# Fused two-problem attention: x0 and K0 loaded in halves, first Q in four PSUM banks, zero matmuls, other slots for Wq, Wo and the output projection, last stores from SP

## The chip, the cores and the metric

One core of one Trainium2 chip runs the whole kernel. The metric is the device time of one execution in microseconds (us). The kernel before takes 1211.83 us, the median of 3 runs (1210.99 to 1212.95). TensorE is called PE, VectorE DVE, ScalarE ACT, GpSimd POOL, SyncE SP.

## The reference

Two independent problems, A and B, of the same shape, are computed one after the other; the outputs stand side by side. Cut to what matters (each of A and B):

```python
B, Sq, D, H, Sk, Dh = 16, 144, 448, 16, 512, 256
q = (x @ wq).reshape(B, Sq, H, Dh).transpose(0, 2, 1, 3)
scores = einsum("bhqd,bhkd->bhqk", q, k_cache) * Dh ** -0.5
p = softmax(scores)
o = einsum("bhqk,bhkd->bhqd", p, v_cache)
out = o.transpose(0, 2, 1, 3).reshape(B, Sq, H * Dh) @ wo
```

All inputs and the output are bf16. K and V of both problems are 268 MB, so the kernel streams them once from HBM while PE computes.

## The kernel before, in words

**Units.** One unit is one (problem, batch, head): 256 units of A, then 256 of B. For each unit the kernel computes Q (L316, eight matmuls over four blocks of D, into the PSUM bank `qp_ps`), moves it to SBUF as `qt_sb` with the factor 1/16 (DVE L328 or ACT L332, by a pattern of the unit number), the scores, the softmax, its transposition, P times V (L511) and an ACT copy of the result into a ring in SBUF (L526).

**The 144 query rows are split 112 + 32.** The 112 rows of one unit are the "a" part: scores SA (L424), maximum (DVE L436), exponential (ACT L447), reciprocal (L457), normalisation (POOL L465), transposition TA (L478) and its copy (L488). The last 32 rows of four units fill 128 partitions together, the "b" part: SB (L348) does eight units at once, into two banks, with its own maximum, exponential, normalisation (L389) and transposition TB (L401).

**Loads.** K comes eight units at a time (one "K load", K0 to K63, 2.1 MB) by a transposing DMA into one of three buffers (L291). V comes four units at a time (V0 to V127, 1 MB) into one of three buffers (L301). x comes four batches at a time by two transposing DMAs (L281, L282) into one of three buffers. Wq comes in four groups of four heads (two DMAs each, L260 and L262) and B's groups overwrite A's; Wo comes in eight groups (L270). All of these are issued by SP, in one order. The stores of the output (L578) are issued by POOL.

**The output projection OP** (L549) takes the ring in chunks of 128 rows (18 chunks for each problem) and adds 32 products for each chunk ("pieces", one matmul each) into `op_ps`; ACT or DVE copies the result out (L567, L570) and the store follows. The ring holds four chunks. The last two chunks of B use two banks (`op_ps` and `qp_ps`).

**The order of the work** is written out by a planner at build time. Its loop (L659 to L753) goes through slots i. In slot i it emits, in this order: the DMAs due, exponentials and normalisations of the b part, stores, Q of unit i+15, SB if one is due (K load n has its SB in slot 8n-7), SA of unit i+5, the normalisation of unit i+4, TA of unit i+2, TB, the maxima of the b part, PV of unit i, and then OP pieces, two at a time, as long as a credit lasts. The credit grows by 2.25 pieces in each slot from slot 0 on, and is cut to 4 in slots in which no piece is queued. A chunk is queued in the slot in which its last unit's PV is emitted and is ready two slots later (`OP_DELAY`): A's chunk 0 in slot 17, chunk 1 in slot 33. Each engine runs its own instructions strictly in this order; `S.add` (L44) works out which semaphores an instruction waits for.

**The order of the loads** comes from `plan(lo, deadline, lead, ...)` (L588 to L623): loads are sorted by deadline (in slots), with ties in the order in which they were planned (x, Wq, Wo, K, V); `lo` is the first slot in which the planner may emit it, because by then the last reader of the buffer has been emitted. SP issues the loads in that order and waits at each one for the readers of its buffer. A load that waits holds back all loads behind it. Around the change from A to B (slots 224 to 257) the order before is V58, K30, V59, V60, x4, Wq group 0 of B, K31, V61, Wq 1, V62, Wq 2, K32, V63, Wq 3, V64, K33. At the start it is x0, Wq 0, Wq 1, Wq 2, K0, Wq 3, V0, K1, V1, V2, K2, then V, K and Wo by deadline, Wo between slots 12 and 26.

Of the kernel before, what the change touches and what calls it, by code (L numbers as in the profile page):

```python
# [122 lines left out]
def bass_concat_heads__mha_block_cached__gqa_block_cached__near_ridge_kernel(  # L123
# [38 lines left out]
    LSB = 7  # L162
    NK, NV, NXG = 3, 3, 3
# [3 lines left out]
    KR = 4  # L167
# [8 lines left out]
    with contextlib.ExitStack() as es:  # L176
# [29 lines left out]
        sem_names = list(COMPUTE)  # L206
# [23 lines left out]
        def t_ident():  # L230
            def e1(g):
                return g.memset(ones[:], 1.0)
            S.add(POOL, e1, writes=[("ones", 0)], name="ones")

            def e2(g):
                return g.affine_select(ident[:], ones[:], pattern=[[1, 128]], compare_op=ALU.is_equal,
                                       fill=0.0, base=0, channel_multiplier=-1)
            S.add(POOL, e2, reads=[("ones", 0)], writes=[("ident", 0)], name="ident")

# [35 lines left out]
        def t_load_x(XG):  # L275
            pr, j = divmod(XG, Bn // XB)
            sl = XG % NXG
            x = xs[pr][j * XB:(j + 1) * XB].rearrange("b q d -> (b q) d")

            def e(q):  # L280
                q.dma_start_transpose(xt_sb[:, sl, 0:3, :], x[:, 0:384]).then_inc(sems["xt%d" % sl], 16)  # L281
                return q.dma_start_transpose(xt_sb[:, sl, 3, :], x[:, 320:448]).then_inc(sems["xt%d" % sl], 16)  # L282
            S.add(SP, e, writes=[(("xt", sl), XG)], dma_sem="xt%d" % sl, n_dma=2, name="x%d" % XG)

        def t_load_k(SG):
            pr, r0 = divmod(8 * SG, NU)
            sl = SG % NK
            src = ks[pr].rearrange("b h k d -> (b h k) d")[r0 * SK:(r0 + 8) * SK, :]

            def e(q):  # L290
                return q.dma_start_transpose(kt_sb[:, sl].rearrange("p k d r -> p (k d) r"),  # L291
                                             src.rearrange("(r k) d -> r (k d)", k=KR)).then_inc(sems["kt%d" % sl], 16)
            S.add(SP, e, writes=[(("kt", sl), SG)], dma_sem="kt%d" % sl, name="k%d" % SG)
# [9 lines left out]

        def t_q(U):
# [4 lines left out]
            hg = h // 4  # L309

            def e(t):
                ins = None
                for kc in range(4):
                    for dc in range(2):
                        c0 = h * DH + dc * 128
                        ins = t.matmul(qp_ps[:, dc * SQ:(dc + 1) * SQ], lhsT=wq_sb[:, kc, c0:c0 + 128],  # L316
# [3 lines left out]
            S.add(PE, e, reads=[(("wq", hg), pr), ("wqz", 0), (("xt", xsl), XG)], writes=[("qp", ("q", U))],  # L320
                  banks=["qp"], name="Q%d" % U)

        def t_evac_q(U):
            sl = U % NQT
            src = qp_ps[:, 0:2 * SQ].rearrange("p (c q) -> p c q", c=2)
            if (U - LQ) % 8 in (2, 4, 6, 7):
                def e(v):
                    return v.tensor_scalar(qt_sb[:, sl, :, :], src, 1.0 / 16.0, None, op0=ALU.mult)  # L328
                S.add(DVE, e, reads=[("qp", ("q", U))], writes=[(("qt", sl), U)], banks=["qp"], name="eq%d" % U)
            else:  # L330
                def e(a):
                    return a.activation(qt_sb[:, sl, :, :], src, AF.Copy, scale=1.0 / 16.0)  # L332
                S.add(ACT, e, reads=[("qp", ("q", U))], writes=[(("qt", sl), U)], banks=["qp"], name="eq%d" % U)
# [5 lines left out]
        def t_sb(SG):  # L339
            ksl = SG % NK  # L340

            def e(t):
                ins = None
                for dc in range(2):
                    for jj in range(8):
                        U = 8 * SG + jj
                        j = jj % 4
                        ins = t.matmul(sb_ps[jj // 4][32 * j:32 * j + 32, :].rearrange("q (k r) -> q k r", k=KR),  # L348
                                       lhsT=qt_sb[:, U % NQT, dc, QA:SQ],
                                       rhs=kt_of(U, dc), start=(dc == 0), stop=(dc == 1),  # L350
                                       tile_position=(0, 32 * j))
                return ins
            S.add(PE, e, reads=[(("qt", (8 * SG + jj) % NQT), 8 * SG + jj) for jj in range(8)] + [(("kt", ksl), SG)],
                  writes=[(("sbb", 0), ("s", 2 * SG)), (("sbb", 1), ("s", 2 * SG + 1))], banks=["sb0", "sb1"],
# [61 lines left out]
        def t_sa(U):  # L416
# [11 lines left out]
            S.add(PE, e, reads=[(("qt", U % NQT), U), (("kt", ksl), SG)], writes=[(("sap", bank), ("s", U))],  # L428
# [41 lines left out]
        def t_ta(U):  # L470
            psl = U % NPA
            bank = U % 2
# [10 lines left out]
        def t_evac_pta(U):  # L483
            sl = U % NPT
            bank = U % 2
# [87 lines left out]
        def t_store(r):  # L573
            pr, row0, m = chunk_rows(r)
            sl = r % NOST

            def e(q):
                return q.dma_start(of[row0:row0 + m, pr * D:(pr + 1) * D], ost_sb[0:m, sl, :]).then_inc(  # L578
                    sems["ost%d" % sl], 16)
            S.add(POOL, e, reads=[(("ost", sl), r)], dma_sem="ost%d" % sl, name="st%d" % r)  # L580
# [4 lines left out]
        t_ident()  # L585
        dma_plan = []
# [4 lines left out]
        s_min = -LQ - 24  # L591
        for XG in range(NXGT):
            pr, j = divmod(XG, Bn // XB)
            u_first = pr * NU + j * XB * H
            dl = u_first - LQ
# [5 lines left out]
            plan(lo, dl, 40, t_load_x, XG)  # L601
        for pr in range(NP):
            for hg in range(HG):
                dl = pr * NU + 4 * hg - LQ
                lo = pr * NU - H + 4 * hg + 3 - LQ + 1 if pr > 0 else s_min
                plan(lo, dl, 10 ** 6, t_load_wq, pr, hg)
        for wg in range(NWG):
            plan(s_min, H - 4 + 2 * wg, 10 ** 6, t_load_wo, 0, wg)
        for SG in range(NSG):
            dl = 8 * SG - LSB  # L610
            lo = 8 * (SG - NK) + 7 - LS + 1 if SG >= NK else s_min
            plan(lo, dl, 12, t_load_k, SG)
        for G in range(NG):
            dl = 4 * G
# [27 lines left out]
        OP_RATE = float(NCH * NWO) / NU  # L642
# [16 lines left out]
        while True:  # L659
# [3 lines left out]
            sgi, ph = divmod(i + LSB, 8)  # L663
            do_sb = ph == 0 and 0 <= sgi < NSG
            ga, gb = 2 * sgi, 2 * sgi + 1
            ok = 0 <= sgi < NSG
            if ok and ph == 1:
                t_exp_b(ga)
            if ok and ph == 3:
                t_exp_b(gb)  # L670
            if ok and ph == 2:
                t_recip_b(ga)
                t_norm_b(ga)
            if ok and ph == 4:
                t_recip_b(gb)
                t_norm_b(gb)
            while stores and stores[0][1] <= i:
                t_store(stores.pop(0)[0])
            if do_sb and sgi == 0:
                t_sb(sgi)  # L680
            u = i + LQ
            if 0 <= u < NT:
# [125 lines left out]
```

## Time and profile before

| | |
|---|---|
| median of 3 runs | 1211.83 us (1210.99 to 1212.95) |
| the profiled execution | 1210.82 us |
| its span (first to last instruction) | 1209.1 us |
| PE busy | 1174.4 us, 97% of the span |
| DVE, ACT, POOL busy | 64%, 62%, 56% |
| DMA | 294.15 MB, mean 243 GB/s |
| first matmul | 10.33 us |
| last matmul ends | 1202.5 us |

The span is the time from the first to the last of the program's own instructions; 1.7 us of the execution lie around it. Busy times are sums over the span, so they say which engine is full, and not where a wait is: for this, the waits and the order of time are read stretch by stretch. "Idle before" in a line is the time for which the engine stood still ahead of that instruction, and the name behind the arrow is what ended it.

### The profile page before, as it was taken

What the parts mean: (1) busy time and instruction counts of PE and PEld (TensorE: products, weight loads), DVE (VectorE), ACT (ScalarE), POOL (GpSimd) and SP (SyncE); (2) the same over time, 40 slices, a digit from 0 to 9 for tenths busy, and PEclk for the clock granted to TensorE, in tenths of its full rate; (3) what the DMA queues carried; (4) which work ended last, traced back from release to release, by engine and by line L of the source; (5) the groups of instructions that cost most, each with busy time, mean ns of one, the idle gap of its engine ahead of it and who ended that gap; (6) DMA issues with size and microseconds to landing.
All of it is one profiled execution on the core that took longest, in us unless ns stands there. A gap on an engine that the chain in (4) does not pass through costs nothing.

```text
span 1209.1 us, 33868 instructions
## 1 busy us (share of the span) xinstructions
PE 1174.4 (97%) x13952; PEld 894.2 (74%) x13952; DVE 770.1 (64%) x2179; ACT 753.7 (62%) x2213; POOL 678.5 (56%) x682
## 2 busy tenths in 40 slices
PE   4898999999999999999999999999999999999997
PEld 3676777777777777777777777777777777777765
DVE  1765666666666666666666666666666666666563
ACT  1665666666666666666666666666666666666553
POOL 0555565565555565565555655655655655665553
PEclk9999999999999999999999999999999999999999
DMA  9999999999999999999999999998999999999971
GB/s 249 281 285 289 245 252 225 245 251 247 246 235 237 231 259 226 246 246 232 290 283 282 284 272 265 228 258 225 245 244 236 224 249 244 242 240 234 232 178 47
DMA packets 627033, 294.15 MB, mean 243 GB/s; under 512 B 548416, under 2 KB 556608, under 8 KB 626880
## 3 DMA queue, kind: packets, MB, share of 16 engines
q1 hardware_dynamic: 625152, 287.85, 101.8%
q0 software_dynamic: 1728, 4.13, 1.1%
q8 instruction: 111, 1.82, 0.6%
q14 instruction: 42, 0.34, 0.1%
HBM read 148.90 MB, written 4.13 MB: 127 GB/s over the span
## 4 chain that ended last, share of the span: by engine, by line
PE 90%; DMA 5%; DVE 3%; SPq 1%; ACT 0%; issue 0%; POOL 0%; ACTq 0%
PE qp_ps L316 20%; PE ot_ps L511 19%; PE sa_ps L424 19%; PE op_ps L549 17%; PE sa_ps L478 8%; PE sb_ps L348 5%; DMA kt_sb<-in_A_k_cache_dram 3%; PE sb_ps L401 2%; DMA kt_sb<-in_B_k_cache_dram 2%; DVE stat L436 1%; DMA wq_sb<-in_A_wq_dram 0%; DVE pt_sb L488 0%; PE qp_ps L549 0%; DVE pt_sb L410 0%; DVE qt_sb L328 0%
## 5 line engine op out<-in xcount | busy, mean ns | idle before, releaser
L465 POOL TENSOR_TENSOR pa_sb<-pa_sb,stat 112x512 bf16<-112x512 bf16 x512 | 531.8, 1039 | 490.8 <-DVE stat L457 490.7
L447 ACT ACTIVATE pa_sb<-sa_ps,stat 112x512 bf16<-112x512 f32 x512 | 352.1, 688 | 408.0 <-DVE stat L436 407.0
L436 DVE TENSOR_REDUCE stat<-sa_ps 112x1 f32<-112x512 f32 x512 | 353.9, 691 | 324.6 <-PE sa_ps L424 321.1
L316 PE MATMUL qp_ps<-xt_sb,wq_sb 128*128 128x144 bf16 x4096 | 344.1, 228 | 16.1 <-DMA wq_sb<-in_A_wq_dram 10.3
L316 PEld LDWEIGHTS qp_ps<-xt_sb,wq_sb 128*128 128x128 bf16 x4096 | 290.5, 99 | 93.1 <-issue 11.1
L511 PE MATMUL ot_ps<-pt_sb,v_sb 128*128 128x144 bf16 x4096 | 340.4, 226 | 0.0
L424 PE MATMUL sa_ps<-kt_sb,qt_sb 128*112 128x512 bf16 x1024 | 310.9, 385 | 1.0 <-DVE pt_sb L488 0.8
L549 PE MATMUL op_ps<-wo_sb,ring 128*128 128x448 bf16 x1120 | 278.8, 352 | 0.0
L511 PEld LDWEIGHTS ot_ps<-pt_sb,v_sb 128*128 128x128 bf16 x4096 | 268.5, 97 | 0.4
L478 PEld LDWEIGHTS sa_ps<-ident,pa_sb 112*128 112x128 bf16 x2048 | 145.0, 97 | 111.3 <-ACT pa_sb L447 24.9
L526 ACT ACTIVATE ring<-ot_ps 128x288 bf16<-128x288 f32 (+8 forms) x512 | 190.3, 372 | 4.4 <-PE ot_ps L511 4.4
L488 DVE COPY pt_sb<-sa_ps 128x448 bf16<-128x448 bf16 x512 | 190.7, 372 | 2.4 <-PE sa_ps L478 2.4
L478 PE MATMUL sa_ps<-ident,pa_sb 112*128 112x112 bf16 x2048 | 185.4, 212 | 0.1
L328 DVE TENSOR_SCALAR qt_sb<-qp_ps 128x288 bf16<-128x288 f32 x256 | 117.0, 457 | 96.5 <-PE qp_ps L316 93.9
L389 POOL TENSOR_TENSOR pb_sb<-pb_sb,stat 128x512 bf16<-128x512 bf16 x128 | 132.8, 1037 | 27.1 <-DVE stat L381 27.1
L332 ACT ACTIVATE qt_sb<-qp_ps 128x288 bf16<-128x288 f32 x256 | 106.0, 414 | 35.0 <-PE qp_ps L316 32.5
L424 PEld LDWEIGHTS sa_ps<-kt_sb,qt_sb 128*112 128x112 bf16 x1024 | 97.0, 129 | 38.8 <-issue 26.7
L549 PEld LDWEIGHTS op_ps<-wo_sb,ring 128*128 128x128 bf16 x1120 | 95.1, 98 | 27.6 <-ACT ring L526 0.2
L447 ACT ACTIVATION_READ_ACCUMULATOR pa_sb<-sa_ps,stat 112x1 f32 x512 | 98.9, 193 | 0.0
L361 DVE TENSOR_REDUCE stat<-sb_ps 128x1 f32<-128x512 f32 x128 | 87.2, 681 | 3.7 <-PE sb_ps L348 3.7
L371 ACT ACTIVATE pb_sb<-sb_ps,stat 128x512 bf16<-128x512 f32 x128 | 88.5, 691 | 0.0
L457 DVE RECIPROCAL stat<-stat 112x1 f32<-112x1 f32 x512 | 78.4, 153 | 0.5 <-ACT pa_sb L447 0.5
(23 smaller groups left out, 366.1 us busy)
## 6 DMA issues: line engine op xcount, KB each, us to landing
v_sb<-in_A_v_cache_dram SPq DMA_DIRECT2D x64, 1024.0 KB, 6.1
v_sb<-in_B_v_cache_dram SPq DMA_DIRECT2D x64, 1024.0 KB, 6.0
out_dram<-ost_sb POOLq DMA_DIRECT2D x36, 112.0 KB, 5.1
wo_sb<-in_A_wo_dram SPq DMA_DIRECT2D x8, 448.0 KB, 6.3
wo_sb<-in_B_wo_dram SPq DMA_DIRECT2D x8, 448.0 KB, 6.2
wq_sb<-in_A_wq_dram SPq DMA_DIRECT2D x4, 768.0 KB, 6.7
wq_sb<-in_B_wq_dram SPq DMA_DIRECT2D x4, 768.0 KB, 7.6
wq_sb<-in_A_wq_dram SPq DMA_DIRECT2D x4, 128.0 KB, 6.9
```

The lines of the kernel that those rows point to most:

```text
L316: ins = t.matmul(qp_ps[:, dc * SQ:(dc + 1) * SQ], lhsT=wq_sb[:, kc, c0:c0 + 128], rhs=xt_sb[:, xsl, kc, xo:xo + SQ], start=(kc == 0 and dc ...
L328: return v.tensor_scalar(qt_sb[:, sl, :, :], src, 1.0 / 16.0, None, op0=ALU.mult)
L389: return g.tensor_tensor(pb_sb[:, psl, :], pb_sb[:, psl, :], stat[:, RINVB + sl:RINVB + sl + 1].to_broadcast([128, SK]), op=ALU.mult)
L424: ins = t.matmul(sa_ps[bank][0:QA, :].rearrange("q (k r) -> q k r", k=KR), lhsT=qt_sb[:, U % NQT, dc, 0:QA], rhs=kt_of(U, dc), start=(dc = ...
L436: return v.tensor_reduce(stat[0:QA, NEG + sl:NEG + sl + 1], sa_ps[bank][0:QA, :], axis=AX.X, op=ALU.max, negate=True)
L447: return a.activation(pa_sb[0:QA, psl, :], sa_ps[bank][0:QA, :], AF.Exp, bias=stat[0:QA, NEG + sl:NEG + sl + 1], scale=1.0, accum_out=stat ...
L465: return g.tensor_tensor(pa_sb[0:QA, psl, :], pa_sb[0:QA, psl, :], stat[0:QA, RINV + sl:RINV + sl + 1].to_broadcast([QA, SK]), op=ALU.mult)
L478: ins = t.transpose(pta_ps[bank][:, c * 128:c * 128 + QA], src[:, c, :], ident[0:QA, 0:QA])
L488: return v.tensor_copy(pt_sb[:, sl, :, 0:QA], pta_ps[bank][:, 0:512].rearrange("p (c q) -> p c q", c=4)[:, :, 0:QA])
L511: ins = t.matmul(ot_ps[ob][:, dc * SQ:(dc + 1) * SQ], lhsT=v_sb[:, vsl, j, c * DH + dc * 128:c * DH + (dc + 1) * 128], rhs=pt_sb[:, sl, c, ...
L526: ins = a.activation(ring[:, 2 * h:2 * h + 2, c0:c0 + n1], src[:, :, 0:n1], AF.Copy)
L549: ins = t.matmul(acc[0:m, 0:D], lhsT=ring[:, c, col0:col0 + m], rhs=wo_sb[:, c, :], start=(c == first), stop=(c == last))
```

## The change

- **Loads at the start.** x0 and K0 are loaded in two halves each, with semaphores of their own for the first halves. The order becomes x0 first half, Wq 0, K0 first half, Wq 1, K0 second half, V0, Wq 2, Wq 3, K1, V1, V2, K2, V3, Wo 0, Wo 1, V4, x0 second half, K3, V5, Wo 2, Wo 3, V6, K4, Wo 4, Wo 5, V7, V8, Wo 6, Wo 7, K5, V9 and so on.
- **Q of the first units.** Units 0 to 7 use four PSUM banks in turn, units 8 to 31 two; the slots of the first 32 Q are set by a table, as are those of SB0, SB1, SB2 (slots -5 and -1, 4, 10) and SA of unit 8 (slot 4). SB0 is split in two.
- **Zero matmuls.** 12 matmuls on zeros ahead of the first Q and 8 behind the first four, into a bank that nothing else uses then.
- **Wq of B** gets the deadlines 232, 236, 240 and 244 in place of 241, 245, 249 and 253. Sorted, the order around the change from A to B becomes V57, Wq 0, V58, K30, Wq 1, V59, Wq 2, V60, x4, K31, Wq 3, V61, V62, K32, V63, V64, K33.
- **Output projection.** A's chunks are ready in slot 34 at the earliest; the credit grows by 2.5 in each slot.
- **Last stores.** The two last chunks are stored by SP with semaphores of their own, and SP waits for them at its end.

```diff
+    WO_AT = (15, 21, 27, 33)
+    OP_FROM = (34, 0)
+    N_WARM = (12, 8)
...
+        def t_warm_zero():
+            def e(v):
+                return v.memset(pt_sb[:, 0, :, :], 0.0)
+            S.add(DVE, e, writes=[("warm", 0)], name="warmz")
...
+        def q_bank(U):
+            four = ((qp_ps, "qp", "qp"), (op_ps, "opp", "op"), (ot_ps[0], ("otp", 0), "ot0"),
+                    (ot_ps[1], ("otp", 1), "ot1"))
+            if U < 8:
+                return four[U % 4]
+            return four[U % 2] if U < 32 else four[0]
...
+        def t_warm(k):
+            def e(t):
+                ins = None
+                for _ in range(N_WARM[k]):
+                    ins = t.matmul(sb_ps[1][:, :], lhsT=ident[:, :], rhs=pt_sb[:, 0, :, 0:128], start=True, stop=True)
+                return ins
...
-            S.add(POOL, e, reads=[(("ost", sl), r)], dma_sem="ost%d" % sl, name="st%d" % r)
+            S.add(SP if r in tail_chunks else POOL, e, reads=[(("ost", sl), r)], dma_sem=sem, name="st%d" % r)
...
+        sb_slot = [8 * n - LSB for n in range(NSG)]
+        sb_slot[0:3] = [-LS, 4, 10]
+        sa_slot = [u - LS for u in range(NT)]
+        sa_slot[8] = 4
+        q_slot = [u - LQ for u in range(NT)]
+        q_slot[0:32] = [-5] * 4 + [-3, -3, -2, -2] + [1] * 4 + [2] * 4 + [4, 5, 5, 6, 7, 8, 9, 9] + \
+            [10, 11, 11, 12, 13, 14, 15, 16]
...
+            if XG == 0:
+                plan(s_min, -60, 0, t_load_x, 0, (0,))
+                plan(s_min, q_slot[2 * H], 40, t_load_x, 0, (1,))
...
-                dl = pr * NU + 4 * hg - LQ
+                dl = pr * NU - H + 4 * hg + 7 - LQ if pr > 0 else (-59, -57, -55, -53)[hg]
                 lo = pr * NU - H + 4 * hg + 3 - LQ + 1 if pr > 0 else s_min
...
-            plan(s_min, H - 4 + 2 * wg, 10 ** 6, t_load_wo, 0, wg)
+            plan(s_min, WO_AT[wg // 2], 10 ** 6, t_load_wo, 0, wg)
...
+            if SG == 0:
+                plan(s_min, -58, 0, t_load_k, 0, (0,))
+                plan(s_min, -56, 0, t_load_k, 0, (1,))
...
-            dl = 4 * G
+            dl = 4 * G if G > 0 else -55.5
...
-        OP_RATE = float(NCH * NWO) / NU
+        OP_RATE = 10.0 / 9 * NCH * NWO / NU
...
-                            queue_chunk(r, i + OP_DELAY)
+                            queue_chunk(r, max(i + OP_DELAY, pr * NU + OP_FROM[pr]))
...
+                if eng_name == SP:
+                    for k in range(len(tail_chunks)):
+                        eng.wait_ge(sems["ostt%d" % k], 16)
```

## The prediction

> **What bounds the kernel now.** I read the chain that ended last, the waits of PE, the stretches of the start, the order of time around the change from A to B, and the end.
>
> ```profile
> PE 90%; DMA 5%; DVE 3%; SPq 1%; ACT 0%; issue 0%; POOL 0%; ACTq 0%
> ```
>
> PE sets the time. An edit pays where PE stands idle and costs where it makes PE wait. PE's waits of over 0.3 us, by cause:
>
> ```profile
> PE qp_ps L316 <- DMA wq_sb<-in_A_wq_dram: 10.3, 1, 10.3
> PE sb_ps L348 <- DMA kt_sb<-in_A_k_cache_dram: 6.1, 4, 1.9
> PE qp_ps L316 <- DVE qt_sb L328: 3.1, 6, 0.6
> PE qp_ps L316 <- ACT qt_sb L332: 2.6, 5, 0.6
> PE sb_ps L348 <- DMA kt_sb<-in_B_k_cache_dram: 2.9, 2, 2.2
> ```
>
> The four K waits in A are SB2 to SB5, at 56.49, 73.76, 94.47 and 112.87 us; the two in B are SB32 and SB33. The stretches between the first six of these SBs (span, PE, PEld, DVE, ACT, POOL, clock, DMA share, GB/s):
>
> ```profile
> 23.60:39.00 15.40, 12.43 (x128) 7.93 (x128) 8.93 (x24) 7.27 (x21) 6.61 (x7) 1.00 1.14 271
> 39.00:56.40 17.40, 15.75 (x201) 11.89 (x200) 11.89 (x35) 11.95 (x36) 10.76 (x11) 1.00 1.19 277
> ...
> 94.40:112.80 18.40, 16.48 (x206) 12.60 (x206) 11.94 (x34) 11.61 (x33) 10.91 (x11) 1.00 1.15 284
> ```
>
> The DMA share is above 1 in all of them, and SP issues without a pause until 125 us. So until SB5 (slot 33) the kernel runs at the pace of the DMA queue, and K5's arrival near 112.8 us is the gate. How many OP pieces PE had done by then:
>
> ```profile
> 0.00:112.87 112.87, 7.69 (x32) 2.78 (x32) 1.00 1.13 272
> 112.87:132.40 19.53, 6.22 (x26) 2.26 (x26) 1.00 1.12 265
> 132.40:148.94 16.54, 1.46 (x6) 0.52 (x6) 1.00 1.20 243
> ```
>
> From SB6 on PE is full. The next place is the reload of Wq. All K loads, issue to landing, and SP around them:
>
> ```profile
> DMA to landing us min/median/max: 11.4/15.2/20.2
> ```
>
> ```profile
> 537.79 7.37 SPq L301 DMA_DIRECT2D v_sb<-in_A_v_cache_dram  x2
> 545.21 12.97 SPq L291 DMA_TRANSPOSE kt_sb<-in_A_k_cache_dram  x1
> ...
> 568.62 0.58 SPq L260 DMA_DIRECT2D wq_sb<-in_B_wq_dram  x1
> 569.24 0.51 SPq L262 DMA_DIRECT2D wq_sb<-in_B_wq_dram  x1
> 569.80 9.92 SPq L291 DMA_TRANSPOSE kt_sb<-in_A_k_cache_dram  x1
> ```
>
> K30 is issued at 545.21, K31 at 569.80. PE at Q243 (slot 228), SB30, Q251 (slot 236) and SB31:
>
> ```profile
> 554.88 0.66 PE L316 MATMUL qp_ps<-xt_sb,wq_sb 128*128 128x144 bf16 x8
> 565.98 1.05 PE L348 MATMUL sb_ps<-kt_sb,qt_sb 128*32 128x512 bf16 x16
> ...
> 572.90 0.66 PE L316 MATMUL qp_ps<-xt_sb,wq_sb 128*128 128x144 bf16 x8
> 583.51 1.05 PE L348 MATMUL sb_ps<-kt_sb,qt_sb 128*32 128x512 bf16 x16
> ```
>
> **The start: nothing is gained by SB5.** Q in four banks takes away the eleven waits for copies (3.1 + 2.6 us); the zero matmuls can let the first Q run at the fast clock (eight cold ones span 1.12 to 1.14 us until 26.5 us, 0.67 us after); the smaller first loads bring Q0 forward by at most x0's second halves, under 1 us. All that stands ahead of K1, and the gate behind it is DMA. By K5 the same bytes must land as before: x0, all of Wq, all of Wo (groups 6 and 7 sort just ahead of K5), K0 to K5, V0 to V8. PE is not the bound: eight slots without OP take 16.54 - 6 x 0.15 = 15.6 us (0.15 us for a piece: 2.99 us less in the third OP row than in the second, for 20 pieces less); from slot 1 at some 28 us, slot 33 could come at 28 + 4 x 15.6, some 90 us. So these edits are worth 0, with some 20 us of idle PE ahead of SB5 as cover; the 20 zero matmuls (128x512, 0.385 us mean, up to double cold, at most 15 us, 12 of them ahead of Q0 in PE's empty 10.3 us) and the memset on DVE (the similar one took 1.76 us) lie in it too. K0 and x0 in parts add three small DMAs and one more change between copies and transposes. No row shows this alone: below nothing if the mix runs better, above two times 1.9 us (a small store, issue to landing). I take **+1.3**.
>
> **OP moved behind slot 33.** Before, 32 pieces are done while PE waits for K. Now none is ready until slot 34. The credit piles up from slot 15 on (a chunk is queued), to 4 + 20 x 2.5 = 54, so chunk 0 comes as a burst of 32 in slot 34, chunk 1 in slots 36 to 38. By slot 49 both kernels have done 64 pieces, so those 32 move from idle PE time to full PE time: 32 x 0.15 = 4.8 to 32 x 0.19 = 6.1 us (ten in a row took 1.89 us). I take **+6.0**. The rate of 2.5 after that moves the same pieces about, on a full PE: 0.
>
> **Wq of B: a new wait on SP.** Wq 0 now stands ahead of V58 and K30 and waits for Q243, its buffer's last reader, which ends at 555.5. Before, nothing held V58 and K30 beyond V58's own buffer, and K30 went at 545.21. Now Wq 0 (0.58 + 0.51), V58 (0.58) go first and K30 is issued near 556.9; SB30 needs it at 565.98, 9.1 us later. Even the shortest landing, 11.4, is late; with the median 15.2 PE waits **+6.1** (bounds 2.3 and 11.1). The same again: Wq 2 waits for Q251, 9.9 us ahead of SB31, and behind it come V60, x4 and K31. Before, the issues of V60, x4 and Wq 0 took from 562.96 to 569.80, so K31 goes some 7 us after Q251, near 580.5, and lands 13.5 later at best of that stretch, 10.5 us late; without the Wq that lay ahead of it then, some 8. I take **+9.0** (6 to 14). Behind it Wq 3, V61, V62 and K32 are one Wq less than before, so the waits of 2.2 and 0.7 us at SB32 and SB33 go: **-2.9**. V60 and x4 land before K31; they add no wait.
>
> **The clock after these waits.** Granted clock at the end (the third number from the right):
>
> ```profile
> 1202.50:1207.50 5.00, 0.03 (x1) 0.00 (x0) 0.62 (x1) 0.29 (x1) 1.12 (x2) 1.00 0.12 46
> 1207.50:1209.10 1.60, 0.00 (x0) 0.00 (x0) 0.00 (x0) 0.00 (x0) 0.00 (x0) 0.51 0.00 0
> ```
>
> The last matmul ends at 1202.5, and 5.0 us later the clock is halved. Waits of 6 and 9 us are longer. At the start some 3.2 us of dense work (SB0 at 23.69 and the Q behind it) passed before Q ran in 0.67 in place of 1.14 us, so a cold start loses 3.2 x (1 - 0.67/1.14) = 1.3 us. Two: **+2.6**, bounds 0 and 6. [...]
>
> **The end.**
>
> ```profile
> L176 POOLq DRAIN  x1: 3006/3006/3006, 1205.9 to 1205.9; - x1
> ```
>
> DVE's last copy ends at 1203.27. POOL issues both stores (1203.09, 1.12 us), they land by 1205.6, then POOL alone needs 3.0 us to drain, and the span ends. With the stores on SP, whose own drain took 0.13 us, POOL's drain follows its last normalisation (1196.04) and is covered by PE's work until 1202.5. SP issues at about 1202.9 and 1203.4, landing 1.9 later as on POOL, plus 0.5: 1205.9. **-3.2**; bounds -3.4 and -0.2 (POOL's median landing of 5.1). SP's queue is empty then. [...]
>
> **Sum.** 1.3 + 6.0 + 6.1 + 9.0 - 2.9 + 2.6 - 3.2 = +18.9. On the profiled execution: 1210.82 + 18.9 = 1229.7. The median of the runs lies 1.0 above it: **1230.7**.
>
> **Rivals.**
> 1. *The shorter start reaches the end.* K5 lands some 7 us earlier, for instance because copies and transposes disturb each other less. For: 23.6 us pass before SB0. Against: same bytes, queue full. 1230.7 - 7 = 1224.
> 2. *The Wq waits are hidden:* K30 and K31 arrive in time. Then 6.1, 9.0 and 2.6 go: 1213. Against: no K landed within 11.4 us.
> 3. *Faster: K lands faster.* One mechanism: a K landing in its shortest 11.4 us and no longer in some 18 (SB2 to SB5 before), because smaller groups of copies stand ahead. Place: the queue up to K5, then K30 and K31. K5 would come when PE is ready, up to 18 us earlier, PE's floor there being some 95; the mid waits become 2.3 and some 7: -18 + 6.0 + 9.3 - 2.9 - 3.2 = -8.8, so 1203. Between 18 and 11.4 the sum turns negative near 13.5. Against: the rows of 271 to 284 GB/s show no gaps to be filled.
> 4. *Worse:* K30 and K31 take the longest landings (11 + 14), SB5 starts cold too: 1230.7 + 10 + 2 = 1243.
> That the change doesn't do what it says is not one of them: the order of loads follows from its deadlines.
>
> **Chances.** Forecast 0.62, rival 1 0.13, rival 2 0.10 (half of it within 0.2%, half above), rival 3 0.08, rival 4 0.07. Two runs' medians can be told apart from about 0.2% on. So faster 0.08, same 0.05, slower 0.87. The range takes in rivals 1 and 4 and the lower bounds of the mid waits, and leaves out rival 3 and part of 2: 1215 to 1243.
>
> **What would show it.** SB5 at 112 to 116 us with no OP ahead of it, and 30 or more OP matmuls in a row behind it; SP waiting before B's first Wq until Q243; PE waits on K of 2 us or more at SB30 and 6 or more at SB31, none at SB33; Q in 1.1 us just after them; two stores on SP and a span that ends some 2.6 us after DVE's last copy. An SB5 before 108 us, or K30 landing before SB30, would make the forecast wrong.

## The result and the profile after

The changed kernel takes 1240.48 us, the median of 5 runs (1239.3 to 1241.8), beside 1212.38 us (5 runs, 1210.99 to 1214.93) for the kernel before. The ratio is 1.0231, with a 95% interval of 1.0216 to 1.0246: it is 28 us slower. The forecast was 1230.7 us, 18.9 us slower. The profiled execution takes 1241.8 us with a span of 1240.1 us, 31.0 us more than the one before. It is the slowest of its kernel's runs, and the profiled one before lies below all five of its own, so the 31.0 us that are split up below are 2.9 more than the medians differ by. Line numbers move: in the changed kernel Q is L339, SB L381, SA L455, TA L509, PV L542, OP L580, the zero matmuls L367, K loads L307, V loads L316, Wq L268 and L270, stores L610.

The chain that ended last, by engine:

```profile
PE 87%; DMA 6%; SPq 3%; DVE 3%; issue 0%; ACT 0%; POOL 0%; DVEq 0%
```

PE's share fell from 90% to 87%, and SP's queue, at 1% before, now has 3%: some of the way to the end leads through SP's issues. PE's waits for DMA (the view of waits: engine, tile and line, what ended the wait, then us in total, times, longest):

```profile
PE sb_ps L381 <- DMA kt_sb<-in_A_k_cache_dram: 25.1, 6, 6.5
...
PE qp_ps L339 <- DMA wq_sb<-in_A_wq_dram: 3.9, 3, 2.6
...
PE qp_ps L339 <- DMA xt_sb<-in_B_x_dram: 2.4, 1, 2.4
...
PE ot_ps L542 <- DMA v_sb<-in_A_v_cache_dram: 1.6, 1, 1.6
```

K of A cost 6.1 us of waits before and 25.1 now: 12.7 of these stand ahead of SB30 and SB31, the other 12.4 at the start. The 10.3 us for the first Wq, in which PE stood empty before, are gone from this row, since the zero matmuls stand there; the last two rows are new. The order of time of PE at the places that matter (start, duration, operation, then in brackets the idle time before it and what ended it):

```profile
111.74 1.90 PE L381 MATMUL sb_ps<-kt_sb,qt_sb 128*32 128x512 bf16 x16 [2.11 <-DMA kt_sb<-in_A_k_cache_dram]
...
117.13 6.22 PE L580 MATMUL op_ps<-wo_sb,ring 128*128 128x448 bf16 x32
...
566.58 0.66 PE L339 MATMUL qp_ps<-xt_sb,wq_sb 128*128 128x144 bf16 x8
...
585.05 1.90 PE L381 MATMUL sb_ps<-kt_sb,qt_sb 128*32 128x512 bf16 x16 [6.55 <-DMA kt_sb<-in_A_k_cache_dram]
...
593.15 0.66 PE L339 MATMUL qp_ps<-xt_sb,wq_sb 128*128 128x144 bf16 x8
...
603.72 0.67 PE L542 MATMUL ot_ps<-pt_sb,v_sb 128*128 128x144 bf16 x8 [1.64 <-DMA v_sb<-in_A_v_cache_dram]
606.75 1.12 PE L339 MATMUL qp_ps<-xt_sb,wq_sb 128*128 128x144 bf16 x8 [2.37 <-DMA xt_sb<-in_B_x_dram]
614.02 1.90 PE L381 MATMUL sb_ps<-kt_sb,qt_sb 128*32 128x512 bf16 x16 [6.15 <-DMA kt_sb<-in_A_k_cache_dram]
```

The rows are SB5, the burst of chunk 0, Q243, SB30, Q251, the PV that needed V60, the first Q that needed x4, and SB31. SB32 and SB33 have no wait. OP's pieces by stretch (the stretch and its length, then busy us and count of PE and of PEld, which are PE's weight loads, then the granted share of PE's full clock, DMA share, GB/s) show none ahead of SB5 and 64 in the 28 us behind it:

```profile
0.00:111.70 111.70, 0.00 (x0) 0.00 (x0) 0.95 1.12 274
111.70:140.00 28.30, 12.76 (x64) 6.12 (x64) 0.94 0.74 179
```

SP's queue at the reload of Wq: first what its Wq loads waited for (the view of waits), then its order of time:

```profile
SPq L268 <- PE qp_ps L339: 25.1, 2, 16.1
```

```profile
567.28 0.37 SPq L268 DMA_DIRECT2D wq_sb<-in_B_wq_dram  x1
567.69 0.51 SPq L270 DMA_DIRECT2D wq_sb<-in_B_wq_dram  x1
568.24 1.50 SPq L316 DMA_DIRECT2D v_sb<-in_A_v_cache_dram  x1
569.78 13.15 SPq L307 DMA_TRANSPOSE kt_sb<-in_A_k_cache_dram  x1
...
593.84 0.37 SPq L268 DMA_DIRECT2D wq_sb<-in_B_wq_dram  x1
594.25 0.50 SPq L270 DMA_DIRECT2D wq_sb<-in_B_wq_dram  x1
594.79 0.59 SPq L316 DMA_DIRECT2D v_sb<-in_A_v_cache_dram  x1
595.43 5.39 SPq L292 DMA_TRANSPOSE xt_sb<-in_B_x_dram  x1
600.86 2.86 SPq L293 DMA_TRANSPOSE xt_sb<-in_B_x_dram  x1
603.76 8.07 SPq L307 DMA_TRANSPOSE kt_sb<-in_A_k_cache_dram  x1
```

The two waits are those for Q243, which ends at 567.24, and for Q251, which ends at 593.81. K30 (569.78) and K31 (603.76) each go out behind a Wq that had waited for its buffer's last Q; K31 has V60 and x4 ahead of it too, and x4 alone holds the queue for 8.3 us.

Where the 31 us arise is read by comparing the start of each SB in both traces, at SBs ahead of which both have done equally many OP pieces:

```
place    pieces done   before     after     lag      grown since the row above
SB7            64      148.94    156.32    + 7.4     + 7.4  start, OP moved
SB29          448      547.81    558.14    +10.3     + 3.0  nothing but the rate of OP
SB33          512      622.30    651.6     +29.3     +19.0  reload of Wq
SB61         1024     1131.04   1165.5     +34.5     + 5.2  nothing but the rate of OP
end of span           1209.1    1240.1     +31.0     - 3.5  last stores
```

The forecast had +7.3, 0, +14.8 with the clock, 0 and -3.2 in these rows. Two of them are off: the reload by 4 us and the rate by 8.

### The profile page after: what moved, and what is told of

The parts are those of the page before. It is cut to its first block, busy times and chain, and to the rows that moved or that the text cites. A ratio compares the mean times of both kernels' runs of the same rounds, so it can differ in the third digit from the quotient of the medians.

```text
span 1240.1 us, 33914 instructions
## 1 busy us (share of the span) xinstructions
PE 1195.1 (96%) x13972; PEld 893.8 (72%) x13972; DVE 771.5 (62%) x2180; ACT 747.9 (60%) x2213; POOL 676.3 (55%) x680
## 4 chain that ended last, share of the span: by engine, by line
PE 87%; DMA 6%; SPq 3%; DVE 3%; issue 0%; ACT 0%; POOL 0%; DVEq 0%
PE sa_ps L455 19%; PE ot_ps L542 18%; PE qp_ps L339 18%; PE op_ps L580 17%; PE sa_ps L509 7%; DMA kt_sb<-in_A_k_cache_dram 6%; PE sb_ps L381 5%; PE sb_ps L432 2%; DVE stat L467 1%; SPq L307 1%; SPq L292 1%; DVE pt_sb L519 1%; DVE pt_sb L441 1%; PE qp_ps L580 0%; SPq L293 0%
## 5 line engine op out<-in xcount | busy, mean ns | idle before, releaser
L542 PE MATMUL ot_ps<-pt_sb,v_sb 128*128 128x144 bf16 x4096 | 341.6, 226 | 1.6 <-DMA v_sb<-in_A_v_cache_dram 1.6
L339 PE MATMUL qp_ps<-xt_sb,wq_sb 128*128 128x144 bf16 x3952 | 328.8, 226 | 6.5 <-DMA wq_sb<-in_A_wq_dram 3.9
L339 PEld LDWEIGHTS qp_ps<-xt_sb,wq_sb 128*128 128x128 bf16 x3952 | 276.0, 98 | 65.5 <-DMA wq_sb<-in_A_wq_dram 5.4
L455 PE MATMUL sa_ps<-kt_sb,qt_sb 128*112 128x512 bf16 x1024 | 316.1, 391 | 1.6 <-DVE pt_sb L519 1.4
L542 PEld LDWEIGHTS ot_ps<-pt_sb,v_sb 128*128 128x128 bf16 x4096 | 269.6, 98 | 2.2 <-DMA v_sb<-in_A_v_cache_dram 1.8
L580 PE MATMUL op_ps<-wo_sb,ring 128*128 128x448 bf16 x1120 | 265.4, 353 | 0.0
L509 PEld LDWEIGHTS sa_ps<-ident,pa_sb 112*128 112x128 bf16 x2048 | 140.6, 97 | 120.3 <-ACT pa_sb L478 46.1
L509 PE MATMUL sa_ps<-ident,pa_sb 112*128 112x112 bf16 x2048 | 186.3, 213 | 1.5 <-ACT pa_sb L478 1.1
L352 DVE TENSOR_SCALAR qt_sb<-qp_ps 128x288 bf16<-128x288 f32 x243 | 111.0, 457 | 87.2 <-PE qp_ps L339 84.3
L455 PEld LDWEIGHTS sa_ps<-kt_sb,qt_sb 128*112 128x112 bf16 x1024 | 96.8, 130 | 49.8 <-issue 30.1
L580 PEld LDWEIGHTS op_ps<-wo_sb,ring 128*128 128x128 bf16 x1120 | 98.2, 98 | 42.9 <-ACT ring L557 0.2
L381 PE MATMUL sb_ps<-kt_sb,qt_sb 128*32 128x512 bf16 x1024 | 71.4, 401 | 27.3 <-DMA kt_sb<-in_A_k_cache_dram 25.1
```

The lines of the kernel that those rows point to most:

```text
L339: ins = t.matmul(acc[:, dc * SQ:(dc + 1) * SQ], lhsT=wq_sb[:, kc, c0:c0 + 128], rhs=xt_sb[:, xsl, kc, xo:xo + SQ], start=(kc == 0 and dc = ...
L381: ins = t.matmul(dst.rearrange("q (k r) -> q k r", k=KR), lhsT=qt_sb[:, U % NQT, dc, QA:SQ], rhs=kt_of(U, dc), start=(dc == 0), stop=(dc = ...
L455: ins = t.matmul(sa_ps[bank][0:QA, :].rearrange("q (k r) -> q k r", k=KR), lhsT=qt_sb[:, U % NQT, dc, 0:QA], rhs=kt_of(U, dc), start=(dc = ...
L509: ins = t.transpose(pta_ps[bank][:, c * 128:c * 128 + QA], src[:, c, :], ident[0:QA, 0:QA])
L542: ins = t.matmul(ot_ps[ob][:, dc * SQ:(dc + 1) * SQ], lhsT=v_sb[:, vsl, j, c * DH + dc * 128:c * DH + (dc + 1) * 128], rhs=pt_sb[:, sl, c, ...
L580: ins = t.matmul(acc[0:m, 0:D], lhsT=ring[:, c, col0:col0 + m], rhs=wo_sb[:, c, :], start=(c == first), stop=(c == last))
```

## Experiments

In the table the ratio is that of each kernel's runs to those of the kernel before on the same chip (1212.9 to 1214.0 us), with its 95% interval. Names beginning with "a" start from the changed kernel, those with "b" and "c" from the kernel before.

| run | edit | us | ratio |
|---|---|---|---|
| a1_wq_back | changed kernel, Wq of B in the old order | 1229.62 | 1.0135 (1.0115 to 1.0154) |
| a2_op_early | changed kernel, OP and Wo early again | 1234.77 | 1.0175 (1.0157 to 1.0193) |
| a3_rate_back | changed kernel, rate 2.25 | 1233.58 | 1.0167 (1.0147 to 1.0188) |
| a4_start_and_stores | all three back: start and stores remain | 1211.29 | 0.9980 (0.9967 to 0.9993) |
| a5_no_zero_matmuls | a4 without zero matmuls | 1210.25 | 0.9975 (0.9964 to 0.9986) |
| b1_stores | last stores on SP alone | 1211.45 | 0.9979 (0.9965 to 0.9993) |
| b2_rate_4p5 | rate 4.5 alone | 1262.19 | 1.0399 (1.0372 to 1.0425) |
| b3_wq_even | Wq deadlines evened out | 1216.38 | 1.0020 (1.0006 to 1.0034) |
| b4_spread | two pieces in every slot | 1205.64 | 0.9935 (0.9914 to 0.9956) |
| c2_spread_stores_even | b4, b1 and b3 | 1203.09 | 0.9910 (0.9883 to 0.9937) |
| c3_wq3_earlier | c2, last Wq earlier | 1201.97 | 0.9901 (0.9872 to 0.9931) |
| c4_fill | b4, b1 and a backlog spent at the reload | 1195.71 | 0.9840 (0.9825 to 0.9856) |

### Taking the parts back one at a time

**a1_wq_back** gives Wq of B its old deadlines again:

```diff
-                dl = pr * NU - H + 4 * hg + 7 - LQ if pr > 0 else (-59, -57, -55, -53)[hg]
+                dl = pr * NU + 4 * hg - LQ if pr > 0 else (-59, -57, -55, -53)[hg]
```

> The changed kernel with one edit: B's Wq groups get the deadlines of before (241, 245, 249, 253). Theory (SP waits at Wq 0 and Wq 2 for Q243 and Q251, and V58, K30, V60, x4 and K31 stand behind them): from SB29 to SB33 the changed kernel lost 19.0 us (10.3 behind before at SB29, 29.3 at SB33), and this comes back, so 1240.5 - 19 = 1221.5; K waits at SB30 and SB31 gone, about 2.9 us at SB32 and SB33 again. Rival (the reload's 3.7 MB are what delays K, wherever they stand in the order): under 5 us come back, 1236 or more.

Some 12 us come back in the runs, not 19. SB30 has no wait any more, but SB31 and its neighbours do (PE's order of time):

```profile
579.51 1.05 PE L381 MATMUL sb_ps<-kt_sb,qt_sb 128*32 128x512 bf16 x16
598.77 1.90 PE L381 MATMUL sb_ps<-kt_sb,qt_sb 128*32 128x512 bf16 x16 [3.39 <-DMA kt_sb<-in_A_k_cache_dram]
621.33 1.05 PE L381 MATMUL sb_ps<-kt_sb,qt_sb 128*32 128x512 bf16 x16 [0.58 <-DMA kt_sb<-in_B_k_cache_dram]
638.42 1.05 PE L381 MATMUL sb_ps<-kt_sb,qt_sb 128*32 128x512 bf16 x16 [1.22 <-DMA kt_sb<-in_B_k_cache_dram]
```

From SB29 to SB33 its lag still grows by 4.7 us (11.4 to 16.1). At rate 2.5 only 2 pieces lie between SB30 and SB31, where the kernel before has 14. So PE gets to SB31 sooner, and K31, which stands behind V59 and V60 and these behind earlier PVs, lands only at 598.63. So rate and reload are not independent, and the expectation, which took the terms for additive, missed.

**a2_op_early** and **a3_rate_back** take back the floor of slot 34 (with Wo's old slots) and the credit:

```diff
-    OP_FROM = (34, 0)
+    OP_FROM = (0, 0)
...
-            plan(s_min, WO_AT[wg // 2], 10 ** 6, t_load_wo, 0, wg)
+            plan(s_min, H - 4 + 2 * wg, 10 ** 6, t_load_wo, 0, wg)
```

```diff
-        OP_RATE = 10.0 / 9 * NCH * NWO / NU
+        OP_RATE = float(NCH * NWO) / NU
```

> The changed kernel with A's chunks ready two slots after their last PV again (no floor of slot 34) and Wo's deadlines of before (12 to 26), which the earlier pieces need. Theory (32 pieces done while PE waits for K before SB5 are free): the 8.5 us lost between SB5 and SB7 come back apart from the cold start at SB5, so 1240.5 - 7 = 1233.5, with SB5 within 3 us of 111.7. Rival (Wo's groups ahead of K3 and K4 make these late, so that what OP gains the K waits take): 1239 or more, with SB5 at 115 or later.

> The changed kernel with the credit of before (2.25 in each slot). Theory (a slot without OP pieces takes 1.78 us, one with two 2.01, and each two more 0.38, so the first two pieces of a slot cost 0.15 us less than others, and each slot left empty loses 0.15): the planner leaves 186 slots empty at 2.5 and 115 at 2.25, so 71 x 0.15 = 10.6 us at most, some 8 after the slots that lie in waits: 1240.5 - 9 = 1231.5. Rival (the prediction's: PE is full, and the rate moves the same pieces about): 1240.5; the lag that grows from SB7 to SB29 and from SB33 to SB61 then has another cause.

Both came out within about 2 us. With OP early, SB5 comes at 114.70 (3.0 later than in the changed kernel, with 32 pieces already done) and the lag at SB7 is 2.0 us instead of 7.4. Wo's place was taken back together with OP's, so the two are not told apart. With the old rate the lag stands still: +7.93 at SB7 and +7.88 at SB29, +25.4 at SB33 and +25.6 at SB61. So the rate alone makes the drift, on an engine that both profiles show as full. Windows from SB7 to SB29, first of the kernel before, then of the changed one (the columns as above, with DVE, ACT and POOL behind PEld):

```profile
148.94:547.81 398.87, 398.57 (x4785) 304.95 (x4786) 263.83 (x748) 258.19 (x766) 232.50 (x232) 1.00 1.05 242
```

```profile
156.32:558.14 401.82, 401.42 (x4784) 303.84 (x4785) 264.01 (x748) 256.14 (x766) 232.50 (x233) 1.00 1.04 240
```

The same work on every engine, PE busy for all but 0.3 and 0.4 us, and 2.95 us more in the second. The busy share doesn't show this: it is 99.9% in both. The weight loads for TA do: their waits for ACT's exponential, in the view of waits, of the kernel before, of the changed one, of a3, and of b2 and b4 below, which have many and few slots without pieces:

```profile
PEld sa_ps L478 <- ACT pa_sb L447: 24.9, 88, 0.6
```

```profile
PEld sa_ps L509 <- ACT pa_sb L478: 46.1, 155, 1.6
```

```profile
PEld sa_ps L509 <- ACT pa_sb L478: 27.2, 91, 1.6
```

```profile
PEld sa_ps L478 <- ACT pa_sb L447: 84.0, 305, 0.6
```

```profile
PEld sa_ps L478 <- ACT pa_sb L447: 7.2, 27, 0.3
```

The slots without pieces in these five kernels are 102, 186, 115, 357 and 26, and the waits stand in them: 83 of the 102 in the kernel before and 150 of the 186 in the changed one have one, of the slots with pieces 2 and 3. One of them, in a stretch of the changed kernel without pieces (PEld's order of time):

```profile
594.20 0.22 PEld L509 LDWEIGHTS sa_ps<-ident,pa_sb 112*128 112x128 bf16 x4 [0.28 <-ACT pa_sb L478]
```

I also took the time from each PV to the next in the trace of PE, for slots without SB or TB, and its median by the number of OP pieces between them (12 from the changed kernel, the others from the kernel before; its two slots with 8 lie at the end, where no Q is left):

```
pieces in the slot      0       2       4       6       10      12
us from PV to PV      1.781   2.010   2.389   2.766   3.524   3.902
```

From 2 pieces on, each pair costs 0.378 us. The first pair costs 0.229. So a slot without pieces loses 0.149 us. With the waits above, I read this as PE's own work there being shorter than the chain SA, maximum (DVE), exponential (ACT), TA, copy (DVE), next SA, whose steps use the two `sa_ps` banks in turn. In the two stretches in which nothing but the spread of OP's pieces differs, the empty slots, their difference from the kernel before times 0.149 us, and the growth of the lag (us) go together in each of these kernels (b4 does two pieces fewer in the first stretch):

```
                  SB7 to SB29                  SB33 to SB61
          empty   x 0.149    lag       empty   x 0.149    lag
before      36                           19
a3          36       0.0    - 0.1        19       0.0    + 0.2
changed     57     + 3.1    + 3.0        58     + 5.8    + 5.2
b2         125     +13.3    +13.9       154     +20.1    +20.6
b4           0     - 5.4    - 5.0         0     - 2.8    - 2.6
```

**a4_start_and_stores** takes back all three (the two diffs above and that of a1). What remains is the start in halves with its zero matmuls, and the stores.

> The changed kernel with B's Wq deadlines, the floor of slot 34, Wo's deadlines and the credit all as before, so that what is left of the change is the start (halves, slots, four banks, zero matmuls) and the last stores. Theory (K5 is the gate in both, the start gains nothing by SB5 and the split adds 1 to 2 us of DMA time): SB5 at 113 to 115 us, SB7 some 2 us behind before, the end 3.5 us shorter: 1.5 us below before, ratio 0.999. Rival (the earlier first Q reaches the end once the losses are gone): SB5 and SB7 some 5 us ahead of before, ratio 0.993.

The time held: 0.998. SB5, behind the same 32 pieces as before, comes at 114.28, 1.40 us late, and SB7 is late by as much. So the start alone gains nothing by SB5, as forecast, although SB0's first half begins at 13.04 us here and SB0 at 23.69 before. The reason given did not hold in this profile. K5 is issued at 95.15 and lands 15.0 us later, at 110.17, 2.6 us ahead of the kernel before. PE is not there: it is busy throughout, and SB5 has no wait (a window, all engines, then PE's order of time):

```profile
94.00:112.00 18.00, 18.00 (x231) 13.99 (x227) 12.93 (x38) 11.92 (x34) 11.01 (x12) 1.00 1.17 304
```

```profile
114.28 1.05 PE L381 MATMUL sb_ps<-kt_sb,qt_sb 128*32 128x512 bf16 x16
```

The waits for K have moved ahead and become fewer and longer: 3.99 us at SB1 and 4.18 at SB3, each followed by 6.83 us at half the clock, where the kernel before has four of 1.1 to 1.9 us at SB2 to SB5 and no half clock behind them. So PE's cover ahead of SB5 is used up; in a5, where K5 lands at 113.76, SB5 does wait for it. From SB29 to SB33 this profile loses 2.3 us more, with a wait of 3.87 us at SB32 (2.19 before, 2.90 in b1, which loads as before).

**a5_no_zero_matmuls** also takes out the zero matmuls (PE then does nothing ahead of Q0):

```diff
-            if i == q_slot[0]:
-                t_warm(0)
...
-            if i == q_slot[0]:
-                t_warm(1)
```

> As a4_start_and_stores, without the 20 zero matmuls. Theory (they only warm a stretch that lies ahead of a K wait of 4 us at SB1): same SB1, SB2 and SB3 to 0.5 us, same time within 1 us as a4_start_and_stores, with the first Q in 1.1 us in place of 0.67. Rival (without them the clock stays cold until 26 us as in before and SB1 or SB2 come late): 2 to 5 us more.

The first Q takes 1.12 us instead of 0.67, as expected. SB2 and SB3 come 1.1 and 1.7 us earlier than in a4, not within 0.5; the changed kernel and a1, with the same program up to there, differ by 1.3 and 1.4 us at these places, so this tells nothing. In time the two intervals overlap almost wholly (0.9967 to 0.9993 and 0.9964 to 0.9986): no effect of the zero matmuls can be told from none. The other parts of the start (halves, banks, slots) were not tested one by one.

### One part alone, on the kernel before

**b1_stores** (the two stores' semaphores and SP's wait for them at its end are not shown):

```diff
...
-            S.add(POOL, e, reads=[(("ost", sl), r)], dma_sem="ost%d" % sl, name="st%d" % r)
+            S.add(SP if r in tail_chunks else POOL, e, reads=[(("ost", sl), r)], dma_sem=sem, name="st%d" % r)
...
```

> The kernel before with the last two stores on SP and nothing else. Theory (POOL's drain of 3.0 us ends the span of before; on SP it is covered): 3.5 us less, 1212.4 - 3.5 = 1208.9. Rival (a store from SP takes longer to land than on POOL, or the drain follows all the same): within 0.5 us of before.

2.5 us are gained in the runs (0.0021 of 1213.6, by the interval 0.8 to 4.2); 3.5 were expected and lie within. In the profiled execution the end saves 3.6 us, but SB63 is 1.1 us late: 0.4 us of it arises before SB5, and the wait at SB32 is 2.90 instead of 2.19. Neither can come from a store at the end, so single profiles scatter by about 1 us here. The end itself is read in the changed kernel: DRAINs (duration in ns, start in us), then SP's stores.

```profile
L179 POOLq DRAIN  x1: 3756/3756/3756, 1229.7 to 1229.7; - x1
```

```profile
1237.42 0.83 SPq L610 DMA_DIRECT2D out_dram<-ost_sb  x2
```

POOL's drain of 3.76 us is over at 1233.5, while PE still has matmuls until 1237.1. The two stores land at 1239.12 and 1239.59, 1.7 us after their issue, and the span ends 0.5 us later.

**b2_rate_4p5** exaggerates the rate:

```diff
-        OP_RATE = float(NCH * NWO) / NU
+        OP_RATE = 2.0 * NCH * NWO / NU
```

> The kernel before with the credit doubled to 4.5 pieces in each slot, nothing else. Theory (each slot without pieces loses 0.15 us, since the first two pieces of a slot cost 0.23 us together and any further two 0.38): the planner leaves 357 slots empty in place of 102, 255 x 0.15 = 38 us more, ratio 1.031. Rival (the prediction's: on a full PE the rate moves the same pieces about): within 1 us of before.

The direction and most of the size held (49 us instead of 38). What the expectation left out is at the start (PE's order of time): at this rate OP asks for Wo before it has come.

```profile
82.84 0.55 PE L549 MATMUL op_ps<-wo_sb,ring 128*128 128x448 bf16 x2 [1.19 <-DMA wo_sb<-in_A_wo_dram]
...
97.09 1.67 PE L549 MATMUL op_ps<-wo_sb,ring 128*128 128x448 bf16 x4 [9.08 <-DMA wo_sb<-in_A_wo_dram]
```

That makes SB5 11.2 us late; from there to SB61 the lag grows by 39.6 us, of which one wait of 3 us is for K31. Of its slots 357 have no pieces, 255 more than before: 255 times 0.149 is 38. Stretch by stretch it agrees too (the table under a3).

**b3_wq_even** tests whether evenly placed Wq groups take away the waits at SB32 and SB33:

```diff
-                dl = pr * NU + 4 * hg - LQ
+                dl = (235, 239, 246, 253)[hg] if pr > 0 else 4 * hg - LQ
```

> The kernel before with B's Wq deadlines 235, 239, 246 and 253, so that Wq 0 stands behind K30, Wq 1 behind V59, Wq 2 behind V61, Wq 3 behind V63: two groups are loaded earlier than before, but none ahead of a K load that is due sooner than the Q it waits for lets through. Theory (it is the place ahead of V58, K30 and K31 that hurts, not the early load): no wait at SB30 and SB31 over 0.5 us, the wait of 2.2 us at SB32 gone, since one Wq group less lands between K31 and K32: 2 to 3 us less than before, ratio 0.998. Rival (any earlier load of Wq delays K, because the DMA queue is full there): waits of 2 us or more at SB30 or SB31, ratio 1.002 or more.

The rival held: the kernel becomes slower, by 0.2% (0.06 to 0.34%). The waits at SB32 and SB33 go, and one of 5.16 us at SB31 takes their place (PE's order of time):

```profile
589.92 1.90 PE L348 MATMUL sb_ps<-kt_sb,qt_sb 128*32 128x512 bf16 x16 [5.16 <-DMA kt_sb<-in_A_k_cache_dram]
```

K31 lands at 589.79. In the kernel before it lands at 583.31, 0.2 us ahead of SB31: there was no slack for one more Wq group in front of it. By the trace of SP, V59 has gone by 561.4, Wq 1 goes out at 565.14, when its Q is done, and V60 behind it at 566.10; before, V60 went at 562.96, which is 564.3 with the 1.3 us by which this run is late already. So some 1.8 us go to Wq 1 on SP. The larger part is behind it: the issue of x4 takes 10.1 us instead of 5.2. Wq 0 and Wq 1, 1.8 MB, now stand ahead of x4, where before none did; that this is the reason is likely, but no run shows it by itself.

### Versions that use what was found

**b4_spread** gives every slot two pieces, and four where more than 34 are ready:

```diff
-                credit += OP_RATE
+                credit = 2.0 + (2.0 if sum(1 for x in fifo["op"] if x[2] <= i) > 34 else 0.0)
...
-                            op_hold = i + 2
+                            op_hold = i + 1
```

> The kernel before with two pieces in every slot in which any is ready, four when more than 34 wait, and the next chunk one slot after the last in place of two. Theory of the empty slots: 26 slots stay empty in place of 102, 76 x 0.15 = 11.3 us less, some of these in the tail where PE waits anyway, so 10 us less, ratio 0.992. Rival (a chunk that follows one slot after the last waits for the copy out of the bank, up to 0.5 us at each of 36 chunks, and fuller slots are no shorter): no gain, ratio 1.00 or above.

It gains 8 us (10 were expected); only 26 slots stay empty. By SB31 it is 5.8 us ahead, and then loses part of it in a wait of 4.3 us at SB32, with half the clock behind it (SB32 takes 1.90 us instead of 1.05): K32 lands 21.3 us after its issue (20.2 before), and PE is there sooner.

**c2_spread_stores_even** joins b4, b1 and b3, and **c3_wq3_earlier** changes its last deadline from 253 to 250.

> The kernel before with three edits: b4_spread's OP, the last stores on SP, and b3_wq_even's deadlines. Theory (the three act at different places: empty slots all along, the end, and the reload): b4's 7.8, 3 for the stores, and the 4.3 us wait that b4 had at SB32 with its cold start, some 4: 1212.9 - 15 = 1198, ratio 0.988. Rival (b4's shorter slots leave the DMA queue less time per K, and K waits appear at SB31 and SB33 in place of that at SB32): ratio 0.991 or more.

> As c2_spread_stores_even, with the last Wq group one step earlier (deadline 250, behind K32 and ahead of V63). Theory: Wq 3 waits for Q255, which is done by then, so it moves 0.9 MB ahead of V63 without a wait: within 1 us of c2_spread_stores_even, less if SB33 waits there. Rival: V63 comes late for its PV, 1 us or more longer.

c2 stayed short of 0.988, at the 0.991 of its rival, since it waits at SB31 (2.15) and SB32 (2.46) instead of at SB32 alone: moving the loads moved the wait. c3 can't be told from c2.

**c4_fill** leaves the loads as before and changes what PE does meanwhile: one chunk of OP more is held over and spent at four pieces per slot while Wq is loaded (slots 233 to 256), and in the tail. The last stores are those of b1 (not shown).

```diff
...
-                credit += OP_RATE
-            if i >= u_tail0 - 14:
+                fill = 233 <= i < 257 or i >= 481
+                thr = 2 if fill else (66 if 129 <= i < 233 or 385 <= i < 481 else 34)
+                credit = 2.0 + (2.0 if sum(1 for x in fifo["op"] if x[2] <= i) > thr else 0.0)
+            if i >= u_tail0:
...
-                            op_hold = i + 2
+                            op_hold = i + 1
```

> The kernel before with its last stores on SP's queue, and with two pieces of the output projection in every slot; a backlog of one chunk more is held over (66 ready pieces instead of 34 in slots 129 to 232 and 385 to 480) and spent at four per slot in slots 233 to 256, where Wq is loaded again and TensorE waited 4.3 us for K at SB32 of the spread run, and from slot 481. Wq's deadlines for the second sequence are those of before. If TensorE's waits there can be filled with work that is ready: the spread's gain of 8 us, 3 us from the stores, some 4 us from the wait and its cold start, 1 us in the tail; about 1198 us beside a before of 1213, ratio 0.987. Rival: pieces in the slots ahead of SB32 only make these slots longer and K lands later by as much, because SP issues it behind a wait that moves with them: the wait at SB32 stays at 3 to 4 us, about 1202 us, ratio 0.991.

It is the fastest of all: 1195.71 us, 18 us below the kernel before, and by the two ratios some 47 us below the changed one. SB31, SB32 and SB33 in PE's order of time:

```profile
576.00 1.05 PE L348 MATMUL sb_ps<-kt_sb,qt_sb 128*32 128x512 bf16 x16
596.67 1.05 PE L348 MATMUL sb_ps<-kt_sb,qt_sb 128*32 128x512 bf16 x16
615.25 1.05 PE L348 MATMUL sb_ps<-kt_sb,qt_sb 128*32 128x512 bf16 x16 [0.42 <-DMA kt_sb<-in_B_k_cache_dram]
```

K32 is issued at 575.11 and lands at 596.05, 20.9 us later; in b4 it was issued at 578.37 and landed 21.3 us later. The transfer is no faster. It went out 0.9 us ahead of SB31, not 0.6 us behind it, and PE had 20.7 us of work between SB31 and SB32 instead of 17.7. The rival, by which K would move along with PE, fell. The run came out some 2 to 4 us below its forecast; 2.2 of that lie after SB33, where it gains 4.8 us by SB63 and b4 2.6. By the ratios it gains some 9 us more than b4 and b1 together (0.0160 against 0.0065 and 0.0021, of 1213); no run has these two without the backlog.

## Why the prediction was right in direction and too low in size

**OP moved and the start (+6.0 and +1.3): right in sum, in part by luck.** The lag is +7.4 by SB7, but it is made otherwise. SB5 came 1.1 us ahead of the kernel before, where the forecast had it 1.3 behind, and from SB5 to SB7 8.5 us were lost, where it had 6.0; the two errors cancel. That K5's arrival is the gate held in the changed kernel (K5 lands at 111.61), but the "some 20 us of idle PE ahead of SB5 as cover" were not all there: in a4 and a2, with the pieces done early, PE comes to SB5 after K5 has landed (in a5 it waits 2.65 us for it). So the 32 pieces were not free. With them early again (a2), SB5 comes 3.0 us later and the way from there to SB7 takes 36.2 us instead of 44.6: the move costs 8.4 us behind SB5 and gives back 3.0 ahead of it, 5.4 in all (6.8 us of the time in its runs: 0.0056 of 1213). The start's own +1.3 is too small to be read: a4 has +1.4 in its one profile, while kernels with the same program up to SB5 differ there by up to 1.1 us (111.74, 111.82 and 112.84 in the changed kernel, a1 and a3), and in the runs a4 (0.9980) gains as much as the stores alone, b1 (0.9979). What the forecast left out of the sum is that SB5 started cold. The wait ahead of it is 2.11 us, and the windows around it read:

```profile
108.32:111.73 3.41, 1.32 (x22) 1.15 (x20) 1.31 (x4) 1.64 (x5) 1.07 (x2) 1.00 1.11 255
111.73:115.15 3.42, 3.41 (x25) 1.61 (x26) 0.44 (x1) 0.00 (x0) 0.00 (x0) 0.50 1.05 394
115.15:118.50 3.35, 3.35 (x38) 2.50 (x36) 2.60 (x9) 2.83 (x8) 2.07 (x3) 1.00 1.19 265
```

Half the clock for 3.41 us loses some 1.7 us (an estimate from the granted 0.50: half of it), of the 2.5 that SB5 to SB7 took beyond the forecast.

**The rate of 2.5 ("the same pieces about, on a full PE: 0"): this is the step that failed.** It cost 8.1 us in the two stretches of the trace in which nothing else differs, and 7.8 us by a3 (0.0064 of 1213). I took a PE that is 100% busy for one that is full, so that only the number of pieces counts. Their place counts as well: a slot without pieces loses 0.15 us to the chain through DVE and ACT.

**Wq of B (+6.1, +9.0, -2.9, clock +2.6, together +14.8): the mechanism was right, the size 4 us too low.** K30's wait came out at 6.55 us, K31's at 6.15, and the waits at SB32 and SB33 are gone. "V60 and x4 land before K31; they add no wait" was wrong as to the wait: PE stood 1.64 us for V60 and 2.37 us for x4, ahead of K31's wait, so the delay by what waits behind Wq 2 is 10.2 us in three pieces, in place of 9.0 in one. The clock cost more than 2.6 us:

```profile
577.00:582.77 5.77, 1.50 (x16) 0.95 (x13) 0.74 (x4) 1.55 (x5) 1.04 (x1) 1.00 1.26 218
582.77:589.60 6.83, 4.55 (x32) 2.54 (x33) 1.58 (x4) 0.85 (x4) 0.74 (x1) 0.50 1.06 289
606.66:616.90 10.24, 4.00 (x28) 1.96 (x29) 0.00 (x0) 0.41 (x1) 0.00 (x0) 0.50 1.12 284
```

From SB30 at 585.05 to 589.60 PE runs at half the clock (0.50 granted): SB 1.90 instead of 1.05 us, PV 1.17 instead of 0.67. That is 4.55 us of work which takes some 2.3 at the full clock (an estimate, half of it), so 2.3 us for the first cold start alone, against 1.3. The second stretch begins with the Q behind x4; the work in it ahead of SB31 lies in time that PE would have waited, and from SB31 at 614.02 to 616.90 another 1.4 us are lost (half of it again). That is 3.7 in place of 2.6. So the 4.2 us are 0.5 for K30, 1.2 behind Wq 2, 1.1 for the clock, and 1.5 for the rate again: a3, with the old rate, grows by 17.5 us from SB29 to SB33 in place of 19.0. The price of the rate in this stretch is not one number, since the edits overlap: a1, a2 and a3, each alone, give back 11.6, 6.8 and 7.8 us, 26.2 in all, while all three at once (a4) give back 30.4 (0.0251 of 1213).

**The end (-3.2): right.** It is -3.5 from SB61 on in the trace, and -2.5 in the runs of b1, whose interval takes in both.

**Rivals.** A start that reaches the end, hidden Wq waits and faster K landings all fell; that copies and transposes disturb each other, as rival 1 supposed, no run shows by itself. K landed 15.0 us after its issue as a median, 15.2 before. But the 11.4 us that stood against rival 2 are no lower bound: K31 landed 10.1 us after its issue (603.76 to 613.89). Of the signs named, SB5 at 111.74 lies just ahead of the 112 given, and the Q behind SB30 took 0.66 us and not 1.1, since the half clock had ended at 589.60; the Q behind x4 took 1.12.

## What to carry to other kernels

A PE that read 99.9% busy still lost 0.149 us in each slot without pieces, by my reading to a chain through DVE and ACT; the same count of instructions in a longer stretch showed it (401.82 us instead of 398.87 from SB7 to SB29), and an even spread of OP's pieces closed it (b4 gains 5.0 us there). Where a load can't come earlier, hold work back for the wait rather than move the load: b3 and c2 moved the wait (5.16 us at SB31; 2.15 at SB31 and 2.46 at SB32), c4 filled it (no wait at SB31 and SB32, 0.42 us at SB33). SP issues in order, and a load that waited for its buffer was paid for by the loads behind it: Wq 0 and Wq 2 waited 25.1 us in the changed kernel, and PE then 6.55 us for K30, 1.64 for V60, 2.37 for x4 and 6.15 for K31. So look at what stands behind a load before moving it forward.

## What the runs showed of the hardware that I had not expected

- The granted clock was halved after a wait of only 2.11 us (SB5 above: 0.50 from 111.73 to 115.15), and stayed full after one of 2.90 us (SB32 of b1: 1.00, the SB 1.05 us long). In c2 the wait of 2.15 us at SB31 is followed by an SB of 1.84 us, at 0.52, that of 2.46 us at SB32 by one of 1.05, at 1.00. So here the length of the wait alone didn't decide. In the changed kernel the waits of 4.15 us at SB1 and 4.73 us at SB3 are followed by 3.41 and 6.83 us at half clock. The stretches at half clock in the changed kernel, up to its last matmul, last 3.41, 6.83, 3.41, 6.83 and 10.24 us, one, two or three times 3.41 us. In the 3.41 us just ahead of the half clock at SB5, PE was busy for 1.32 us.
- One more Wq group of 0.9 MB ahead of K31 made it land 6.5 us later in b3 (5.2 without the lag that was there already), most of it in the issue of x4: the transposing x4 takes 5.2 us to issue in the kernel before, with no Wq group ahead of it, 8.3 in the changed kernel and 10.1 in b3, with two ahead of it.
- POOL's drain at the end took 3.0 us before and 3.76 in the changed kernel, though its last two stores had gone to SP (3.76 in c4 too).
